# Running the W1 and wo matmuls as pairs of 64-row tiles, and moving N into the W2 stretches

## The chip, the cores and the metric

The kernel runs on one core of one Trainium2 chip. The metric is device time in microseconds (us), lower is better. PE is TensorE (the matmul engine), PEld its weight loads, ACT ScalarE, DVE VectorE, POOL GpSimd, SP the engine that issues most DMAs. A kernel's time is the median of its runs; single runs of one kernel differ by up to 1.3%, and a good part of this study is about telling such noise from effects.

## The reference

One transformer layer on 2048 rows of width 576, in bf16. First a linear-attention mixer with 32 heads of 18 channels, then a channel MLP of width 4608:

```python
h  = x + A(layernorm(x))          # q, k, v; softmax feature maps; kv and z; num / den; then @ wo
h2 = h + B(layernorm(h))

def A(x):                         # cut: q, k, v per head, phi_q and phi_k are softmaxes of both signs
    num = phi_q @ kv              # "N" below: numerator and denominator of the attention
    den = phi_q @ z + 1e-6
    return (num / den) @ wo       # wo: 576 x 576

def B(x):
    y = layernorm(x)
    return gelu(y @ w1 + b1) @ w2 + b2    # w1: 576 x 4608, w2: 4608 x 576
```

## The kernel before

Rows are taken in 16 tiles of 128 (`t`). After a first phase (keys, values, the kv sums, queries) comes a loop of 8 rounds, `r = 0..7`, each with two tiles. A round has a W1 stretch (36 blocks `m` of hidden units for 256 rows, then gelu on ACT) and a W2 stretch (two tiles). N, wo and the second layernorm of the next round's two tiles, `a` and `b`, are put in between.

The contraction length of W1 and wo is 576 = 4 x 128 + 64. The four full chunks are ordinary 128-row matmuls. The remainder of 64 rows is done in W1 as two 64-row matmuls at a time, one on the upper and one on the lower half of the array (`h = 0` and `h = 64`), and in wo padded with zeros to 128 rows.

```python
def w1_group(r, g, off=0, n=RW):            # four blocks m, two PSUM banks
    b0 = 2 * (g % 2)
    where = [(4 * g + i, b0 + i // 2, 512 * (b0 + i // 2) + RW * (i % 2)) for i in range(4)]
    for i in (0, 2, 1, 3):                  # tails: 64 rows, two at a time
        m, bk, o = where[i]; h = 64 * (i // 2); w = 128 * (2 * g + i % 2)
        P.add("pe", matmul(ps_all[:, o:o + n], w1t[h:h + 64, w:w + 128], yT[h:h + 64, 4, ys], ...), banks=[bank[bk]])
    for m, bk, o in where:                  # full chunks: 128 rows
        for c in range(4):
            P.add("pe", matmul(ps_all[:, o:o + n], w1sb[:, c, 128 * m:128 * m + 128], yT[:, c, ys], ...), banks=[bank[bk]])
    ...                                     # four gelus on ACT

def attn_wo(t, bset, early=False):
    for c in range(5):                      # 512 + 64 output columns, 128 rows
        for (bk, o, n) in ((A, 0, 512), (C, 512, 64)): ...
    ...                                     # DVE: residual, sums; POOL: power; DVE: norm; transposing DMA

def w2_tile(r, j, slots):
    for i in range(NF + LAG):               # NF = 36; per m 512 columns in bank mb, 64 columns in bank 4
        if i in slots: slots[i]()
        ...
    P.add("pool", tmpo = x_all[t] + b2)     # b2 addition, emitted after the tile
    ...                                     # DVE: ostage = PSUM + tmpo; DMA out

for r in range(NR):
    for g in range(NG):
        w1_group(r, g)
        if more and r and g == 0: attn_N(a, S1)
        if more and g == 5:       attn_wo(a, S1)
        if more and g == 6:       attn_N(b, S1)
    slots = {24: attn_wo(b, S1)} if more
    w2_tile(r, 0, slots); w2_tile(r, 1, {})
```

The softmax here doesn't subtract the row's maximum and nothing guards it: scores larger than these inputs give would overflow.

## Time and profile before

| | before |
|---|---|
| time, median of the first 4 runs | 440.04 us (439.58 to 440.81) |
| profiled span | 437.4 us |
| PE busy | 95% |
| a steady round (r = 1 to 6) | 41.10 us |
| of it the W1 stretch (one wo, two N inside) | 21.77 us |
| of it the W2 stretch (one wo inside) | 19.33 us |
| the last round's W1 (nothing inside) | 19.39 us |

A stretch is measured from its first weight load to that of the next stretch. From the page: the span; PE's busy time, share and instructions; the chain of work that ended last, by engine and by line; and two of the costliest groups (L839: full W1 matmuls, L833: W1 tails; columns: busy us and mean ns of one, then idle time before them). In the chain, "issue" is time in which an engine waited for nothing that the profile shows, and a name with q is an engine's sequencer, which issues its instructions.

```profile
span 437.4 us, 8921 instructions
PE 415.1 (95%) x3685; PEld 265.3 (61%) x3685; DVE 186.8 (43%) x461; ACT 183.1 (42%) x406; POOL 94.8 (22%) x120
PE 81%; DVE 10%; issue 3%; ACT 2%; DMA 2%; POOL 1%; SPq 1%; DVEq 0%; ACTq 0%
PE ps_all L839 31%; PE ps_all L862 26%; PE ps_all L833 5%; PE ps_all L684 4%; PE ps_all L599 4%; PE ps_all L534 4%; PE ps_all L519 3%; DVE ybuf L380 2%; PE ps_all L629 2%; DMA RA<-in_A_wqkv_dram 2%; PE ps_all L569 2%; DVE tpn L693 1%; SPq L330 1%; POOL st L701 1%; DVE bns L366 1%
...
L839 PE MATMUL ps_all<-yT,w1sb 128*128 128x256 bf16 x1152 | 138.2, 273 | 0.0
...
L833 PE MATMUL ps_all<-yT,w1t 64*128 64x256 bf16 x288 | 28.2, 274 | 2.0 <-ACT yT L618 2.0
```

PE is the bound, and W1 and W2 are most of it. But "busy" does not say whether a matmul's time was used: the records overlap, one lasts 273 ns while a new one starts every 109 ns. What the groups cost must be read from starts. The timeline of PE in one steady W1 stretch (start us, length us, then line and operation, merged):

```profile
198.15 0.39 PE L833 MATMUL ps_all<-yT,w1t 64*128 64x256 bf16 x4
...
198.47 1.92 PE L839 MATMUL ps_all<-yT,w1sb 128*128 128x256 bf16 x16
...
200.33 0.39 PE L833 MATMUL ps_all<-yT,w1t 64*128 64x256 bf16 x4
```

One group takes 200.33 - 198.15 = 2.18 us. Its matmuls fill 18 slots of 109 ns (16 full ones and two pairs of tails), 1.97 us. The single records show where the other 0.21 us is (ns from start to start):

```
full -> full                 109
last full -> first tail      205     change from 128-row to 64-row matmuls
tail -> other tail of a pair   3     the two halves of the array run together
  -> first tail of next pair 116     or 117; so 119 or 120 from pair to pair
  -> other tail of that pair   3
last tail -> first full      202     change back
first full -> second full    119
```

So each change between 128-row and 64-row matmuls costs about 0.1 us: 93 to 96 ns in its own gap, and 10 or 11 more in the next. There are two per group and 72 groups.

Another cause is at hand: the tails of a group also wait for ACT, which must have emptied their bank, and the view names ACT before many of them. But of the 44 groups that follow a full matmul directly, it names ACT for 31 and nothing for 13, and the gap is the same 0.21 us, as in these two weight loads:

```profile
111.58 0.11 PEld L833 LDWEIGHTS ps_all<-yT,w1t 64*128 64x128 bf16 x4 [0.21 <-issue]
113.76 0.12 PEld L833 LDWEIGHTS ps_all<-yT,w1t 64*128 64x128 bf16 x4 [0.21 <-ACT RA L844]
```

So the gap is not a wait for ACT; experiment 3 tests this without ACT. The Trainium skill, "TensorEngine Tiling (Array Packing)", section "Key Properties", says that a change of tiling mode drains TensorE; the pause at each change in the trace agrees, though it does not show the drain itself, and it gives the size, which the page does not.

### The profile page before, as it was taken

The numbers are of one execution on the slowest core, as the hardware profiler recorded it, in microseconds if no ns is written. First come the engines' busy times: TensorE is split into PE (matmuls) and PEld (weight loads), VectorE is DVE, ScalarE is ACT, GpSimd is POOL, SyncE is SP. The second block draws the span as 40 slices with busy tenths as digits, with TensorE's granted clock in tenths as the row PEclk, the third lists the DMA queues.
The fourth block names the chain that finished last, engine by engine and source line by source line (L and its number), as shares of the span: only waits on it lengthen the run. The fifth ranks groups of instructions, "written<-read, shape, count | busy, mean of one in ns | idle before, by whom it ended". The sixth has DMA issues, their size and how long they took to land.

```text
span 437.4 us, 8921 instructions
## 1 busy us (share of the span) xinstructions
PE 415.1 (95%) x3685; PEld 265.3 (61%) x3685; DVE 186.8 (43%) x461; ACT 183.1 (42%) x406; POOL 94.8 (22%) x120
## 2 busy tenths in 40 slices
PE   6679999886999999999999999999999999999996
PEld 2346666665774576467647755775576567646753
DVE  4598898787053125332334332452135322430000
ACT  1447775376870175026404620660175026404710
POOL 4179783001102111201121012102111201121000
PEclk9889999999999999999999999999999999999999
DMA  8689887400610100310310011101100100110000
GB/s 187 144 174 205 254 190 201 139 1 1 211 38 16 43 16 19 26 30 16 32 30 16 15 31 30 30 15 17 43 17 15 31 28 16 30 30 15 2 0 29
DMA packets 49265, 26.11 MB, mean 60 GB/s; under 512 B 37064, under 2 KB 48200, under 8 KB 49224
## 3 DMA queue, kind: packets, MB, share of 16 engines
q1 hardware_dynamic: 46912, 23.67, 23.4%
q10 hardware_dynamic: 2312, 1.86, 1.7%
q8 instruction: 29, 0.48, 0.5%
q14 instruction: 12, 0.10, 0.1%
HBM read 14.47 MB, written 2.36 MB: 38 GB/s over the span
## 4 chain that ended last, share of the span: by engine, by line
PE 81%; DVE 10%; issue 3%; ACT 2%; DMA 2%; POOL 1%; SPq 1%; DVEq 0%; ACTq 0%
PE ps_all L839 31%; PE ps_all L862 26%; PE ps_all L833 5%; PE ps_all L684 4%; PE ps_all L599 4%; PE ps_all L534 4%; PE ps_all L519 3%; DVE ybuf L380 2%; PE ps_all L629 2%; DMA RA<-in_A_wqkv_dram 2%; PE ps_all L569 2%; DVE tpn L693 1%; SPq L330 1%; POOL st L701 1%; DVE bns L366 1%
## 5 line engine op out<-in xcount | busy, mean ns | idle before, releaser
L844 ACT ACTIVATE RA<-ps_all,b1T 128x256 bf16<-128x256 f32 x288 | 122.5, 470 | 183.8 <-PE ps_all L839 174.1
L839 PE MATMUL ps_all<-yT,w1sb 128*128 128x256 bf16 x1152 | 138.2, 273 | 0.0
L839 PEld LDWEIGHTS ps_all<-yT,w1sb 128*128 128x128 bf16 x1152 | 106.8, 98 | 26.6 <-issue 15.2
L862 PE MATMUL ps_all<-w2a,RA 128*128 128x512 bf16 (+1 forms) x640 | 95.3, 286 | 0.7
L862 PEld LDWEIGHTS ps_all<-w2a,RA 128*128 128x128 bf16 x640 | 46.0, 98 | 38.6 <-DVE WQ L871 4.1
L862 PE MATMUL ps_all<-RB,RA 128*128 128x64 bf16 (+1 forms) x512 | 68.6, 286 | 0.0
L690 DVE SCALAR_TENSOR_TENSOR x_all<-ps_all,x_all 128x576 bf16<-128x576 f32 x16 | 12.1, 756 | 113.6 <-PE ps_all L684 113.6
L862 PEld LDWEIGHTS ps_all<-RB,RA 128*128 128x128 bf16 x512 | 33.5, 98 | 32.3
L871 DVE TENSOR_TENSOR WQ<-ps_all,tmpo 128x64 bf16<-128x64 f32 (+1 forms) x32 | 14.6, 455 | 86.2 <-PE ps_all L862 84.6
L665 POOL TENSOR_TENSOR obuf<-tpn 128x576 bf16<-128x576 f32 x14 | 19.6, 1401 | 110.8 <-DVE tpn L660 110.8
L701 POOL TENSOR_TENSOR st<-st,neghalf 128x1 f32<-128x1 f32 x16 | 8.8, 548 | 155.1 <-DVE st L703 155.1
L833 PE MATMUL ps_all<-yT,w1t 64*128 64x256 bf16 x288 | 28.2, 274 | 2.0 <-ACT yT L618 2.0
L868 POOL TENSOR_TENSOR tmpo<-x_all,b2bc 128x576 f32<-128x576 bf16 x16 | 20.4, 1273 | 43.6 <-DVE WQ L871 43.6
L605 ACT ACTIVATE Eq<-ps_all 128x512 bf16<-128x512 f32 (+1 forms) x48 | 25.3, 527 | 10.4 <-PE ps_all L599 9.5
L380 POOL TENSOR_SCALAR ybuf<-x_all,st 128x576 bf16<-128x576 bf16 x12 | 27.6, 2300 | 1.8 <-POOL st L360 0.9
L525 ACT ACTIVATE RB<-ps_all 128x576 bf16<-128x576 f32 x32 | 19.1, 647 | 20.4 <-PE ps_all L519 20.4
L599 PE MATMUL ps_all<-yT,WQ 128*128 128x256 bf16 x200 | 25.0, 273 | 0.2 <-ACT Eq L605 0.2
L519 PE MATMUL ps_all<-RA,yT 128*128 128x512 bf16 (+1 forms) x160 | 23.1, 293 | 1.4 <-ACT RB L525 1.3
L555 DVE TENSOR_TENSOR RB<-ps_all,RB 128x1152 bf16<-128x1152 f32 x16 | 21.5, 1346 | 6.8 <-PE ps_all L534 6.7
L534 PE MATMUL ps_all<-RB,yT 128*128 128x512 bf16 (+1 forms) x160 | 22.9, 291 | 0.3 <-DVE RB L555 0.3
L684 PE MATMUL ps_all<-wo_sb,OTR 128*128 128x512 bf16 (+1 forms) x160 | 22.2, 286 | 0.1
L544 DVE TENSOR_REDUCE sums<-RB 128x64 f32<-128x1152 bf16 x16 | 21.5, 1341 | 0.0
(86 smaller groups left out, 293.1 us busy)
## 6 DMA issues: line engine op xcount, KB each, us to landing
w1sb<-in_B_w_dram SPq DMA_DIRECT2D x8, 576.0 KB, 4.8
w2a<-in_B_w_dram SPq DMA_DIRECT2D x4, 720.0 KB, 6.8
RB<-in_B_w_dram SPq DMA_DIRECT2D x2, 1152.0 KB, 7.6
out_dram<-WQ SPq DMA_DIRECT2D x16, 144.0 KB, 1.9
x_all<-in_A_x_dram SPq DMA_DIRECT2D x2, 576.0 KB, 4.7
RB<-in_A_wqkv_dram ACTq DMA_DIRECT2D x1, 576.0 KB, 5.8
x_all<-in_A_x_dram ACTq DMA_DIRECT2D x1, 576.0 KB, 7.9
w1t<-in_B_w_dram SPq DMA_DIRECT2D x2, 288.0 KB, 4.0
```

The source lines that it names most:

```text
L380: P.add(eng, lambda e: e.tensor_scalar(ybuf[yb][:, 0:D], src, mean, rstd, ALU.subtract, ALU.mult), reads=[r_src, *r_st], writes=[res(f"ybu ...
L519: P.add("pe", lambda e, c=c, o=o, n=n: e.matmul(ps_all[:, 512 * KB + o:512 * KB + o + n], yT[:, c, sl * 128:(sl + 1) * 128], weffk[:, c, o ...
L534: P.add("pe", lambda e, c=c, o=o, n=n: e.matmul(ps_all[:, 512 * VB + o:512 * VB + o + n], yT[:, c, sl * 128:(sl + 1) * 128], wv[:, c, o:o ...
L544: P.add("dve", lambda e: e.tensor_reduce(sums[vb][:, :], Ek[eb][:, 0:1152].rearrange("p (h f) -> p h f", h=64), AX.X, ALU.add), reads=[res ...
L555: P.add("dve", lambda e: e.tensor_tensor(vx(t)[:, :, :, 0:DH], ps_all[:, 512 * VB:512 * VB + D].rearrange("p (h d) -> p h d", h=H).unsquee ...
L599: P.add("pe", lambda e, i=i, c=c, h0=h0: e.matmul(ps_all[:, 512 * bk + RW * i:512 * bk + RW * i + RW], weffq[:, c, DH * h0:DH * h0 + 128], ...
L605: P.add("act", lambda e, s=s: e.activation(Eq[:, r, s, bs[0]:bs[0] + n, :], ps_all[:, 512 * bk:512 * bk + RW * n].rearrange("p (b t) -> p ...
L684: P.add("pe", lambda e, c=c, bk=bk, o=o, n=n: e.matmul(ps_all[:, 512 * bk:512 * bk + n], oT[ob][:, c, :], wo_sb[:, c, o:o + n], start=(c = ...
L833: P.add("pe", lambda e, i=i, o=o, h=h, w=w: e.matmul(ps_all[:, o:o + n], w1t[h:h + 64, w:w + 128], yT[h:h + 64, 4, ys], start=(i % 2 == 0) ...
L839: P.add("pe", lambda e, c=c, m=m, o=o: e.matmul(ps_all[:, o:o + n], w1sb[:, c, 128 * m:128 * m + 128], yT[:, c, ys], start=False, stop=(c ...
L844: P.add("act", lambda e, m=m, o=o: e.activation(hmid[:, m, off:off + n], ps_all[:, o:o + n], AF.Gelu_apprx_tanh, bias=b1T[:, m:m + 1]), re ...
L862: P.add("pe", lambda e, m=m, bk=bk, o=o, n=n: e.matmul(ps_all[:, 512 * bk:512 * bk + n], w2_lhs(m, j), w2_rhs(m, o, n), start=(m == 0), st ...
```

## The change

The intent: run all of W1 as 64-row matmuls, so that the mode no longer changes inside it. Every 128-row matmul becomes two 64-row ones, on the upper and lower half of the array, that run at once. Two halves at work must not write one PSUM bank (the Trainium skill, same page, "Gotcha 1: PSUM Pressure", says so and leaves it to software), so at any time the two lanes work on unlike units (a unit is two blocks `m` in one bank), and semaphores hold back a lane that takes over a bank from the other. A "takeover" below is that: the first matmul of a lane on a unit whose other half the other lane has just done.

The same is done for wo, whose 576 output columns now lie as 288 + 288 in two banks. Both wo of a round go into W1 (they no longer change the mode there). Both N, whose matmuls are 128-row ones, go from W1 to W2. The core of the diff:

```diff
+    def wo_half(t, bset, step):              # lanes pe0 (rows 0-63) and pe8 (rows 64-127), unlike banks
+        lo = [one("pe0", step, 0, c, ...) for c in cs]
+        hi = [one("pe8", 1 - step, 64, c, ...) for c in cs]      # N=288, 5 + 4 pairs in two steps
@@ attn_N
+        P.add(oeng, obuf[:, 576:640] = tpn[:, 0, 512:576] + tpn[:, 1, 512:576])   # copy of the last 64 columns
@@ W1
-    def w1_group(...)
+    UBANK = ...                              # 18 units over banks 0 to 4
+    SKEW = 3
+    def w1_round(r, extra):
+        for s in range(NF // 2):
+            k = s % 3
+            u8 = s + (2, -1, -1)[k]          # pe0: units 0,1,2,...   pe8: units 2,0,1,...
+            lo += w1_half(r, s, 0, k < 2)
+            hi += w1_half(r, u8, 64, k == 0)
+            ...                              # gelus of finished units; extra: halves of wo
+        hi = [(None, None)] * SKEW + hi      # program order: pe0 matmul i+3, then pe8 matmul i
@@ w2_tile
-        mb = 2 + (RT * r + j) % 2
+        mb = (3, 2)[j]
+        for ... in (64 columns, 512 columns)[::1 - 2 * j]:   # second tile: DVE evicts the 512-column bank first
@@ rounds
+            ia, ib = (3, 12) if r else (9, None)          # wo(a), wo(b): after W1 steps 3, 4 and 12, 13
+            if r == 0:
+                extra[4] = attn_N(b); slots[0][8] = attn_wo(b, S1, True)
+        if r + 2 < NR:
+            slots[0][16 if r == 0 else 2] = attn_N(a + RT)
+            slots[1][6 if r else 12] = attn_N(b + RT)
```

(Shortened; the bookkeeping gives each lane its own semaphore and makes a lane wait for the other where they touch the same bank.)

More of the change, by code (lines that the diff above doesn't have):

```diff
@@ L12 @@
 ENG_PIDS = ("pe", "act", "dve", "pool", "sp")
+LANES = ENG_PIDS + ("pe0", "pe8")
 ENG_ATTR = {"pe": "tensor", "act": "scalar", "dve": "vector", "pool": "gpsimd", "sp": "sync"}
 class Res:
-    __slots__ = ("name", "w", "r", "strict")
+    __slots__ = ("name", "w", "r")
     def __init__(self, name=""):
         self.name = name
-        self.strict = name.startswith("junk")
         self.w = None
@@ L50, in __init__ @@
         self.ops = {p: [] for p in ENG_PIDS}
+        self.lane = {p: [] for p in LANES}
         self.seen = {p: {} for p in ENG_PIDS}
@@ L57, in _need, with _collect @@
             waits[tok[0]] = tok[1]
-    def _collect(self, eng, reads, writes, banks):
+    def _collect(self, lane, reads, writes, banks):
         waits = {}
-        inorder = eng == "pe"
+        pe = lane in ("pe", "pe0", "pe8")
         for r in reads:
@@ L64, in _collect @@
         for w in writes:
-            if w.w is not None and (w.strict or not (inorder and w.w[0] == eng)):
-                self._need(waits, w.w)
-            for pid, v in w.r.items():
-                if not (inorder and pid == eng):
-                    self._need(waits, (pid, v))
+            self._need(waits, w.w)
+            for tok in w.r.items():
+                self._need(waits, tok)
         for b in banks:
             for pid, v in b.last.items():
-                if pid != eng:
+                if {pid, lane} == {"pe0", "pe8"} or not (pid == lane or pe and pid[:2] == "pe"):
                     self._need(waits, (pid, v))
@@ L77, in _plan_waits @@
         for pid, v in sorted(waits.items()):
-            if v <= 0 or (eng == "pe" and pid == "pe"):
-                continue
-            if self.seen[eng].get(pid, 0) >= v:
+            if v <= 0 or self.seen[eng].get(pid, 0) >= v:
                 continue
@@ L83, in _plan_waits @@
             self.seen[eng][pid] = v
-            if pid in ENG_PIDS:
-                self.ops[pid][v - 1].inc_needed = True
+            if pid in LANES:
+                self.lane[pid][v - 1].inc_needed = True
     @staticmethod
@@ L96, in _mark, with add @@
             b.last[tok[0]] = tok[1]
-    def add(self, eng, fn, reads=(), writes=(), banks=()):
+    def add(self, lane, fn, reads=(), writes=(), banks=()):
+        eng = lane[:2] if lane in ("pe0", "pe8") else lane
         op = _Op(fn)
-        self._plan_waits(eng, self._collect(eng, reads, writes, banks), op)
-        op.inc_sem = eng
+        self._plan_waits(eng, self._collect(lane, reads, writes, banks), op)
+        op.inc_sem = lane
         self.ops[eng].append(op)
-        self._mark((eng, len(self.ops[eng])), reads, writes, banks)
+        self.lane[lane].append(op)
+        self._mark((lane, len(self.lane[lane])), reads, writes, banks)
     def chan(self, name, eng):
@@ L134, in emit @@
         vals = {}
-        for pid in ENG_PIDS:
+        for pid in LANES:
             count = 0
             vl = [0]
-            for op in self.ops[pid]:
-                if op.inc_needed and op.inc_sem == pid:
+            for op in self.lane[pid]:
+                if op.inc_needed:
                     count += 1
@@ L155, in body @@
                     for (wpid, wv) in op.waits:
-                        v = vals[wpid][wv] if wpid in ENG_PIDS else wv
+                        v = vals[wpid][wv] if wpid in LANES else wv
                         engine.wait_ge(sems[wpid], v)
@@ L160, in body @@
                     ins = op.fn(engine)
-                    if op.inc_sem in ENG_PIDS:
+                    if op.inc_sem in LANES:
                         if op.inc_needed:
@@ L479, in _build @@
     P.add("dve", lambda e: e.memset(weffq[:, :, 576:592], 0.0), writes=[res("weffqpad"), res("warm")])
-    P.add("dve", lambda e: e.memset(wo_sb[64:128, 4, :], 0.0), writes=[res("wopad")])
-    for i in range(2):
-        P.add("dve", lambda e, i=i: e.memset(obuf[i][:, D:640], 0.0), writes=[res(f"opad{i}")])
     bulk = []
@@ L497, in _build @@
     add_bulk(wo_sb[:, 0:4, :], A_wo[0:512, :].rearrange("(c p) m -> p c m", p=128), [res("wo")])
-    add_bulk(wo_sb[0:64, 4, :], A_wo[512:576, :], [res("wo4")])
+    DHF = D // 2
+    for k in range(2):
+        add_bulk(wo_sb[64 * k:64 * k + 64, 4, 0:DHF], A_wo[512:576, DHF * k:DHF * k + DHF], [res("wo4")])
     NW2A = NF - NW2B
@@ L666, in attn_N @@
               reads=[res("tpn")], writes=[res(f"obuf{ob}")])
+        P.add(oeng, lambda e: e.tensor_tensor(obuf[ob][:, D:640], tpn[:, 0, 512:D], tpn[:, 1, 512:D], ALU.add),
+              reads=[res("tpn")], writes=[res(f"opad{ob}")])
         if oeng == "pool":
@@ L677, in attn_oT, with one @@
             pe_tr(obuf[ob], oT[ob], bset, rd, wr)
+    def wo_half(t, bset, step):
+        A, C, B = bset
+        ob = t % 2
+        def one(lane, k, h, c, first, last):
+            bk = (A, C)[k]
+            o = 0 if c == 4 else DHF * k
+            P.add(lane, lambda e: e.matmul(
+                ps_all[:, 512 * bk:512 * bk + DHF], oT[ob][h:h + 64, c, :], wo_sb[h:h + 64, c, o:o + DHF],
+                start=first, stop=last, skip_group_check=True),
+                reads=[res(f"oT{ob}"), res("wo"), res("wo4")], banks=[bank[bk]])
+        cs = (4, 0, 1, 2, 3) if step == 0 else (0, 1, 2, 3)
+        lo = [lambda c=c: one("pe0", step, 0, c, c == 4, step == 1 and c == 3) for c in cs]
+        hi = [lambda c=c: one("pe8", 1 - step, 64, c, c == 4, step == 1 and c == 3) for c in cs]
+        return lo, hi
     def attn_wo(t, bset, early=False):
         A, C, B = bset
-        ob = t % 2
-        for c in range(5):
-            for (bk, o, n) in ((A, 0, 512), (C, 512, 64)):
-                P.add("pe", lambda e, c=c, bk=bk, o=o, n=n: e.matmul(
-                    ps_all[:, 512 * bk:512 * bk + n], oT[ob][:, c, :], wo_sb[:, c, o:o + n],
-                    start=(c == 0), stop=(c == 4)),
-                    reads=[res(f"oT{ob}"), res("wo"), res("wo4"), res("wopad")], banks=[bank[bk]])
+        if early:
+            for step in range(2):
+                for a, b in zip(*wo_half(t, bset, step)):
+                    a()
+                    b()
         w = res(f"s2_{t}")
@@ L690, in attn_wo @@
         P.add("dve", lambda e: e.scalar_tensor_tensor(
-            x_all[:, t, :], ps_all[:, 512 * A:512 * A + D], 0.0, x_all[:, t, :], ALU.add, ALU.add,
-            accum_out=st(0)), reads=[res(f"x{t}")], writes=[res(f"x{t}"), w], banks=[bank[A], bank[C]])
+            x_all[:, t, :].rearrange("p (k d) -> p k d", k=2),
+            hap(ps_all, PR, 512 * A, [[512 * (C - A), 2], [1, DHF]]), 0.0,
+            x_all[:, t, :].rearrange("p (k d) -> p k d", k=2), ALU.add, ALU.add, accum_out=st(0)), reads=[res(f"x{t}")], writes=[res(f"x{t}"), w], banks=[bank[A], bank[C]])
         P.add("dve", lambda e: e.scalar_tensor_tensor(
@@ L705, in attn_wo @@
         yb = norm("dve", x_all[:, t, :], res(f"x{t}"), st(6), st(5), (res(f"s2f_{t}"), res(f"s2e_{t}")), True)
-        if not early:
+        if t >= RT:
             tr_y(yb, t)
@@ L777, in _build @@
         bulk.pop(0)()
-    ps_kv = lambda off, dims: hap(ps_all, PR, off, dims, 126)
+    ps_kv = lambda off, dims: hap(ps_all, PR, off, dims)
     P.add("dve", lambda e: e.tensor_tensor(
-        kvr[0:126, :, 0:25, 0:19], ps_kv(512 * 5, [[512, 2], [19, 25], [1, 19]]),
-        mask25[0:126, :, :].unsqueeze(1).to_broadcast([126, 2, 25, 19]), ALU.mult),
+        kvr[:, :, 0:25, 0:19], ps_kv(512 * 5, [[512, 2], [19, 25], [1, 19]]),
+        mask25[:, :, :].unsqueeze(1).to_broadcast([128, 2, 25, 19]), ALU.mult),
         reads=[res("mask25")], writes=[res("kvr")], banks=[bank[5], bank[6]])
     P.add("dve", lambda e: e.tensor_tensor(
-        kvr[0:126, :, 25:32, 0:19], ps_kv(512 * 7, [[133, 2], [19, 7], [1, 19]]),
-        mask7[0:126, :, :].unsqueeze(1).to_broadcast([126, 2, 7, 19]), ALU.mult),
+        kvr[:, :, 25:32, 0:19], ps_kv(512 * 7, [[133, 2], [19, 7], [1, 19]]),
+        mask7[:, :, :].unsqueeze(1).to_broadcast([128, 2, 7, 19]), ALU.mult),
         reads=[res("mask7")], writes=[res("kvr")], banks=[bank[7]])
@@ L821, in _build @@
     ch_out = [P.chan(f"out{i}", "sp") for i in range(2)]
-    def w1_group(r, g, off=0, n=RW):
-        b0 = 2 * (g % 2)
-        y0 = yts(r).start + off
-        ys = slice(y0, y0 + n)
-        yr = yrs(r)[off // 128:(off + n) // 128]
-        where = [(4 * g + i, b0 + i // 2, 512 * (b0 + i // 2) + RW * (i % 2)) for i in range(4)]
-        for i in (0, 2, 1, 3):
-            m, bk, o = where[i]
-            h = 64 * (i // 2)
-            w = 128 * (2 * g + i % 2)
-            P.add("pe", lambda e, i=i, o=o, h=h, w=w: e.matmul(
-                ps_all[:, o:o + n], w1t[h:h + 64, w:w + 128],
-                yT[h:h + 64, 4, ys], start=(i % 2 == 0), stop=False, skip_group_check=True),
-                reads=R_w1t + yr, banks=[bank[bk]])
-        for m, bk, o in where:
-            for c in range(4):
-                P.add("pe", lambda e, c=c, m=m, o=o: e.matmul(
-                    ps_all[:, o:o + n], w1sb[:, c, 128 * m:128 * m + 128],
-                    yT[:, c, ys], start=False, stop=(c == 3), skip_group_check=True),
-                    reads=[res(f"w1_{c}_{m // 18}")] + yr, banks=[bank[bk]])
-        for m, bk, o in where:
-            P.add("act", lambda e, m=m, o=o: e.activation(
-                hmid[:, m, off:off + n], ps_all[:, o:o + n], AF.Gelu_apprx_tanh, bias=b1T[:, m:m + 1]),
-                reads=[res("b1T")], writes=[res(f"hm{m}_{j}") for j in range(off // 128, (off + n) // 128)] +
-                (RA_OLD if r == 0 else []), banks=[bank[bk]])
@@ new lines, in _build, with w1_half, one @@
+    UNITS = [(4 * (u // 2) + u % 2, 4 * (u // 2) + u % 2 + 2) for u in range(NF // 2)]
+    UBANK = {}
+    for k in range(0, NF // 2, 3):
+        for i, u in enumerate((k, k + 2, k + 1)):
+            UBANK[u] = (k + i) % 5
+    def w1_half(r, u, h, begin):
+        lane = "pe8" if h else "pe0"
+        ys, yr, bk = yts(r), yrs(r), UBANK[u]
+        def one(i, c, first):
+            m = UNITS[u][i]
+            o = 512 * bk + RW * i
+            if c == 4:
+                w = 128 * (2 * (m // 4) + m % 2)
+                lhs, rd = w1t[h:h + 64, w:w + 128], R_w1t
+            else:
+                lhs, rd = w1sb[h:h + 64, c, 128 * m:128 * m + 128], [res(f"w1_{c}_{m // 18}")]
+            P.add(lane, lambda e: e.matmul(ps_all[:, o:o + RW], lhs, yT[h:h + 64, c, ys],
+                                           start=first, stop=not begin and i == 1 and c == 3, skip_group_check=True),
+                  reads=rd + yr, banks=[bank[bk]])
+        k = 1 if h else 0
+        return [lambda i=i, c=c, n=n: one(i, c, begin and n == 0)
+                for n, (i, c) in enumerate([(k, 4)] + [(i, c) for i in (0, 1) for c in range(4)])]
@@ new lines, in w1_act @@
+    def w1_act(r, u):
+        for i, m in enumerate(UNITS[u]):
+            o = 512 * UBANK[u] + RW * i
+            P.add("act", lambda e, m=m, o=o: e.activation(
+                hmid[:, m, :], ps_all[:, o:o + RW], AF.Gelu_apprx_tanh, bias=b1T[:, m:m + 1]),
+                reads=[res("b1T")], writes=[res(f"hm{m}_{j}") for j in range(RT)] +
+                (RA_OLD if r == 0 else []), banks=[bank[UBANK[u]]])
+    SKEW = 3
+    def w1_round(r, extra):
+        lo, hi = [], []
+        for s in range(NF // 2):
+            k = s % 3
+            u8 = s + (2, -1, -1)[k]
+            lo += [(f, None) for f in w1_half(r, s, 0, k < 2)]
+            hi += [(f, None) for f in w1_half(r, u8, 64, k == 0)]
+            if k == 1:
+                hi.append((None, lambda s=s: w1_act(r, s - 1)))
+            if k == 2:
+                hi.append((None, lambda s=s: (w1_act(r, s), w1_act(r, s - 1))))
+            for fl, fh, after in extra.get(s, ()):
+                lo += [(f, None) for f in fl]
+                hi += [(f, None) for f in fh]
+                if after:
+                    hi.append((None, after))
+        hi = [(None, None)] * SKEW + hi
+        n8 = 0
+        while lo or n8 < len(hi):
+            if lo:
+                f = lo.pop(0)[0]
+                f()
+            while n8 < len(hi):
+                f, g = hi[n8]
+                if f is None and g is not None:
+                    g()
+                    n8 += 1
+                    continue
+                if f is not None:
+                    f()
+                n8 += 1
+                break
+            while n8 < len(hi) and hi[n8][1] is not None:
+                hi[n8][1]()
+                n8 += 1
@@ L869, in w2_tile @@
               reads=[res("b2"), res(f"x{t}")], writes=[res("tmpo"), res("maskf")])
-        for bk, o, n in ((TAILB, 512, 64), (mb, 0, 512)):
+        for bk, o, n in ((TAILB, 512, 64), (mb, 0, 512))[::1 - 2 * j]:
             P.add("dve", lambda e, bk=bk, o=o, n=n: e.tensor_tensor(
@@ L875, in w2_tile @@
               reads=[res(f"ostage{ob}")])
-    NG = NF // 4
     for r in range(NR):
         a, b = RT * (r + 1), RT * (r + 1) + 1
-        more = r + 1 < NR
-        for g in range(NG):
-            w1_group(r, g)
-            if more and r and g == 0:
-                attn_N(a, S1)
-            if more and g == 5:
-                attn_wo(a, S1)
-            if more and g == 6:
-                attn_N(b, S1)
-        slots = {}
-        if more:
-            slots[24] = lambda b=b: attn_wo(b, S1)
-        w2_tile(r, 0, slots)
-        w2_tile(r, 1, {})
+        extra, slots = {}, ({}, {})
+        if r + 1 < NR:
+            ia, ib = (3, 12) if r else (9, None)
+            for t, i in ((a, ia), (b, ib)):
+                if i is not None:
+                    extra[i] = [(*wo_half(t, S1, 0), None)]
+                    extra[i + 1] = [(*wo_half(t, S1, 1), lambda t=t: attn_wo(t, S1))]
+            if r == 0:
+                extra[4] = [((), (), lambda: attn_N(b, S1))]
+                slots[0][8] = lambda: attn_wo(b, S1, True)
+        if r + 2 < NR:
+            slots[0][16 if r == 0 else 2] = lambda: attn_N(a + RT, S1)
+            slots[1][6 if r else 12] = lambda: attn_N(b + RT, S1)
+        w1_round(r, extra)
+        w2_tile(r, 0, slots[0])
+        w2_tile(r, 1, slots[1])
     P.final_dma_waits("sp")
```

## The prediction

> **What bounds the kernel now.** TensorE. The page gives PE 95% of the 437.4 us span; the chain of waits is 81% PE (30.5% full W1 matmuls, 25.5% W2, 5.4% W1 tails). In the waits view PE's stalls (about 18 us in all) lie before the steady rounds. Six steady rounds take 41.1 us each (in the chain, 150.34 to 396.94): in the windows view W1 with one wo and two N takes 21.7, W2 with the other wo 19.3. ScalarE (13.9 of 21.7 in W1) is not the limit.
>
> In the trace's single matmuls, full W1 matmuls start every 109 ns. A group of 16 plus four 64-row tails takes 2.176 us, though 18 slots of 109 are 1.966. The rest is two changes between 128- and 64-row matmuls: about 200 ns from start to start in place of 109, and 10 more in the next gap, near 0.1 us each. The Trainium skill, "TensorEngine Tiling (Array Packing)", Key Properties, says that changing the tiling mode drains TensorE; the 200 ns gaps agree. 72 groups x 0.206 = 14.8 us, all on the critical path.
>
> **What the change does to the sum.**
> - Array work is equal: 9 slots a unit. In the tail pairs the second tile starts 3 ns after the first, both weight loads under the running matmuls. Expected: pairs every 109-112 ns.
> - Removed: 14.8 us of changes. Left per W1 stretch: two changes (8 x 0.2) and a skew of three slots (8 x 0.33): net -10.6.
> - wo: 1.22 us inserted before; now nine paired slots of N=288, about 1.1. 14 in the loop: -1.7.
> - wo out of W2: the gap at the change of W2 tiles (475 ns against 216, behind VectorE's eviction) goes in steady rounds: -1.8.
> - N (0.6 us each) only moves.
> - Lane waits: a dependent matmul comes four slots (436 ns) after the one it needs, whose record lasts 272 ns: free, unless signalling takes over 100 ns.
> - Against it, round 0: wo(3) and N(4) sit in W2 tile 0, N(5) in tile 1. GpSimd runs in order, so the b2 addition (1.27 us) queues behind N's output addition, 6 us after N starts. Estimated stalls: 2.2 us in tile 1, 0.7 in the next W1, 0.4 of extra changes, 0.6 because ScalarE needs 1.99 us per four gelus in round 0 against 1.97 of matmul.
> - Before the loop: 0.4 for the copied columns and mode changes.
>
> Sum: -9.8 us at 109 ns a slot. Each ns above adds 1.3 us; allowing a little, 431.5 us.
>
> **What would show each step.** Single matmuls in W1: pair spacing near 109 ns, no 200 ns gaps inside; W1 stretch near 20.4 us with two wo; W2 near 18.9 with two N; a steady round 39.3 to 39.8. The waits view: a new PE wait of 2-3 us in round 0 for VectorE's eviction (W2's 64-column matmuls). PE waits for its own lanes near zero.
>
> **What would make it wrong.** Instruction delivery: W1 needs a load and a matmul every 54 ns for 18 us on end; before has that pace only in bursts (52.7 ns over 10, 83 over 60). A slot of 120 ns would take all the gain (+14 us). Lane signals slower than 436 ns would stall twelve times a round. Round 0 stalling less would make it faster: about 428.
>
> Chances: faster by over 2% (under 431.6) 0.48, within 2% 0.44, slower 0.08. Range 426 to 438.

## The result

| | before | after |
|---|---|---|
| time, median of 4 runs | 440.04 us | 427.91 us (427.46 to 430.21) |
| ratio after / before | | 0.9733 (95%: 0.9695 to 0.9771) |
| a steady round (after: r = 2 to 5) | 41.10 us | 39.12 us |
| W1 stretch of a steady round | 21.77 us | 20.23 us |
| W2 stretch of a steady round | 19.33 us | 18.90 us |
| the last round's W1 | 19.39 us | 18.02 us |
| first round, W1 and W2 | 21.19, 19.34 us | 20.00, 22.36 us |
| first W1 load to last matmul | 324.4 us | 312.6 us |

Ratios are the mean time of one kernel's fast runs over that of the other's of the same rounds, so they are not quite the ratio of the medians quoted. The kernel became 2.7% faster; 431.5 us was predicted, with a range of 426 to 438. The lines of the page after (L860 is W1, L928 W2, L688 wo):

```profile
span 426.3 us, 11565 instructions
PE 396.8 (93%) x4924; PEld 287.1 (67%) x4965; DVE 182.9 (43%) x460; ACT 175.3 (41%) x406; POOL 98.3 (23%) x134
...
L860 PE MATMUL ps_all<-yT,w1sb 64*128 64x256 bf16 x2304 | 152.2, 269 | 0.0
...
L860 PE MATMUL ps_all<-yT,w1t 64*128 64x256 bf16 x288 | 71.5, 270 | 2.5 <-ACT yT L617 2.0
...
L688 PE MATMUL ps_all<-wo_sb,OTR 64*128 64x288 bf16 x288 | 29.4, 283 | 0.3
```

The number of matmuls on W1's full chunks doubled (1152 to 2304), and PE's busy time fell. The same steady round in both kernels, before and after, in the view by windows (stretch, its length, busy us and count of instructions for PE, PEld, DVE, ACT, POOL, then granted clock, DMA share and GB/s). Before, W1 and W2:

```profile
232.14:253.91 21.77, 21.77 (x213) 16.43 (x211) 10.07 (x33) 13.91 (x34) 1.95 (x2) 1.00 0.11 24
253.91:273.25 19.34, 19.24 (x157) 9.81 (x155) 4.56 (x12) 1.17 (x3) 4.46 (x4) 1.00 0.11 25
```

After:

```profile
231.85:252.08 20.23, 20.23 (x363) 19.04 (x361) 6.13 (x20) 12.38 (x32) 1.09 (x2) 1.00 0.08 20
252.08:270.98 18.90, 18.58 (x161) 10.29 (x165) 7.87 (x24) 1.61 (x5) 5.82 (x6) 1.00 0.14 32
```

The last round's W1, in which nothing is inserted, before and after:

```profile
396.54:415.93 19.39, 19.39 (x182) 14.38 (x180) 0.92 (x2) 13.80 (x34) 1.27 (x1) 1.00 0.03 10
387.19:405.21 18.02, 18.02 (x327) 17.16 (x324) 0.92 (x2) 12.16 (x32) 1.27 (x1) 1.00 0.04 11
```

Weight loads are busy 19.0 of 20.2 us in W1 now, at full clock, and still the pairs start every 109 ns: delivering a load and a matmul every 54 ns for a whole stretch is no limit here. That was the largest risk named.

The new waits of PE in the loop, after (total us, times, longest; one more lies before the loop, for DVE at L412, 1.3 us here and 0.8 us in a second profile of the same kernel):

```profile
PE ps_all L928 <- DVE WQ L937: 1.9, 1, 1.9
...
PE ps_all L928 <- ACT RA L871: 1.1, 7, 0.2
...
PE ps_all L860 <- DVE WQ L937: 0.6, 1, 0.6
```

The first and the last are the stalls of the first round that were predicted. Their cause can be read in the timeline around them, in order of time:

```profile
141.26 1.40 POOL L664 TENSOR_TENSOR obuf<-tpn 128x576 bf16<-128x576 f32 x1 [4.59 <-issue]
142.62 0.32 POOL L666 TENSOR_TENSOR obuf<-tpn 128x64 bf16<-128x64 f32 x1
142.90 1.27 POOL L934 TENSOR_TENSOR tmpo<-x_all,b2bc 128x576 f32<-128x576 bf16 x1
144.30 0.95 DVE L937 TENSOR_TENSOR WQ<-ps_all,tmpo 128x64 bf16<-128x64 f32 x2 [3.17 <-POOL tmpo L934]
144.59 1.67 PE L928 MATMUL ps_all<-w2a,RA 128*128 128x64 bf16 x13 [1.93 <-DVE WQ L937]
```

N's output additions (L664, L666) hold POOL; the b2 addition (L934) stands behind them in POOL's order, although its data had been there all along; DVE's eviction waits for it; and PE waits for the bank.

The middle line of the waits, seven times 0.16 us for ACT at the start of W2, is not real. There the first W2 weight load starts 198 ns after the last W1 matmul, as at any change of mode, and the second load 15 ns later; the first W2 matmul ran between, but its record is missing (the page counts 623 of 640), so the gap looks longer by one matmul.

### The profile page after: what moved, and what is told of

Same layout as the page of the kernel before. It is cut to its first block, busy times and chain, and to the rows that moved or that the text cites. A ratio compares the mean times of both kernels' runs of the same rounds, so it can differ in the third digit from the quotient of the medians.

```text
span 426.3 us, 11565 instructions
## 1 busy us (share of the span) xinstructions
PE 396.8 (93%) x4924; PEld 287.1 (67%) x4965; DVE 182.9 (43%) x460; ACT 175.3 (41%) x406; POOL 98.3 (23%) x134
## 4 chain that ended last, share of the span: by engine, by line
PE 61%; issue 2%; ACT 1%; POOL 1%; DVE 0%; ACTq 0%; DVEq 0%
PE ps_all L928 29%; PE ps_all L860 28%; PE ps_all L688 4%; PE ps_all L628 1%; ACT RA L871 1%; POOL tmpo L934 1%; DVE WQ L937 0%; POOL obuf L664 0%; POOL obuf L666 0%; ACTq L157 0%; DVEq L157 0%
## 5 line engine op out<-in xcount | busy, mean ns | idle before, releaser
L871 ACT ACTIVATE RA<-ps_all,b1T 128x256 bf16<-128x256 f32 x288 | 114.8, 478 | 180.2 <-PE ps_all L860 165.4
L860 PE MATMUL ps_all<-yT,w1sb 64*128 64x256 bf16 x2304 | 152.2, 269 | 0.0
L860 PEld LDWEIGHTS ps_all<-yT,w1sb 64*128 64x128 bf16 x2304 | 135.4, 94 | 6.2
L928 PE MATMUL ps_all<-w2a,RA 128*128 128x64 bf16 (+1 forms) x623 | 93.9, 284 | 3.9 <-DVE WQ L937 1.9
L860 PE MATMUL ps_all<-yT,w1t 64*128 64x256 bf16 x288 | 71.5, 270 | 2.5 <-ACT yT L617 2.0
L928 PEld LDWEIGHTS ps_all<-w2a,RA 128*128 128x128 bf16 x640 | 45.8, 98 | 37.9 <-DVE WQ L937 2.2
L928 PE MATMUL ps_all<-RB,RA 128*128 128x64 bf16 (+1 forms) x499 | 66.7, 284 | 0.4
L928 PEld LDWEIGHTS ps_all<-RB,RA 128*128 128x128 bf16 x512 | 33.4, 98 | 32.4
L707 DVE SCALAR_TENSOR_TENSOR x_all<-ps_all,x_all 128x576 bf16<-128x576 f32 x16 | 12.1, 757 | 83.0 <-PE ps_all L688 83.0
L664 POOL TENSOR_TENSOR obuf<-tpn 128x576 bf16<-128x576 f32 x14 | 19.6, 1401 | 92.3 <-DVE tpn L659 81.2
L934 POOL TENSOR_TENSOR tmpo<-x_all,b2bc 128x576 f32<-128x576 bf16 x16 | 20.3, 1271 | 43.2 <-DVE WQ L937 43.2
L688 PE MATMUL ps_all<-wo_sb,OTR 64*128 64x288 bf16 x288 | 29.4, 283 | 0.3
L860 PEld LDWEIGHTS ps_all<-yT,w1t 64*128 64x128 bf16 x288 | 26.3, 94 | 4.7 <-ACT yT L617 2.1
L524 ACT ACTIVATE RB<-ps_all 128x576 bf16<-128x576 f32 x32 | 19.1, 647 | 20.5 <-PE ps_all L518 20.5
L533 PE MATMUL ps_all<-RB,yT 128*128 128x64 bf16 (+1 forms) x154 | 21.6, 287 | 0.3
```

Of the source, the lines that this page charges most:

```text
L533: P.add("pe", lambda e, c=c, o=o, n=n: e.matmul(ps_all[:, 512 * VB + o:512 * VB + o + n], yT[:, c, sl * 128:(sl + 1) * 128], wv[:, c, o:o ...
L664: P.add(oeng, lambda e: e.tensor_tensor(obuf[ob][:, 0:D], tpn[:, 0, :], tpn[:, 1, :], ALU.add), reads=[res("tpn")], writes=[res(f"obuf{ob}")])
L688: P.add(lane, lambda e: e.matmul(ps_all[:, 512 * bk:512 * bk + DHF], oT[ob][h:h + 64, c, :], wo_sb[h:h + 64, c, o:o + DHF], start=first, s ...
L860: P.add(lane, lambda e: e.matmul(ps_all[:, o:o + RW], lhs, yT[h:h + 64, c, ys], start=first, stop=not begin and i == 1 and c == 3, skip_gr ...
L871: P.add("act", lambda e, m=m, o=o: e.activation(hmid[:, m, :], ps_all[:, o:o + RW], AF.Gelu_apprx_tanh, bias=b1T[:, m:m + 1]), reads=[res( ...
L928: P.add("pe", lambda e, m=m, bk=bk, o=o, n=n: e.matmul(ps_all[:, 512 * bk:512 * bk + n], w2_lhs(m, j), w2_rhs(m, o, n), start=(m == 0), st ...
```

## The experiments

Twelve kernels were run. Two things disturb their total times. One is short: PE's granted clock falls to half for one or a few periods of 3.4 us before the loop and, in some executions, also once at the start of the first W1 stretch. The Trainium skill, "TensorE: Matmul & The Clock Gate", Part 1, describes such a gate with a window of that length; the traces agree, with half-clock periods of 3.41, 6.83 or 10.24 us before the loop. Here is one execution of a kernel met below (early b2, second time), the clock in the third number from the end:

```profile
109.00:113.00 4.00, 2.02 (x26) 1.67 (x24) 3.16 (x11) 3.04 (x6) 0.35 (x1) 1.00 0.01 2
113.00:117.40 4.40, 4.40 (x54) 3.62 (x51) 0.00 (x0) 1.76 (x4) 1.33 (x2) 0.61 0.32 52
```

Where it falls on the first W1 stretch, that takes 21.67 us in place of 20.00. The other is the first weights' DMA, for which PE waited 5.3 to 8.6 us in these profiles. The profile of the kernel before shows both as well (half clock at 13.0 and 26.7 us, and 6.5 us of waiting). So the verdicts below rest on stretches of the loop after the first W1, which repeat to 0.01 us from execution to execution, and the totals are given beside them.

The theories. **A**: the gain is the mode changes that W1 no longer makes; moving wo and N only makes that possible. **B**: the gain is the new place of wo and N, through shorter W2 stretches. **C**: 64-row matmuls are cheaper in themselves; this one the trace of after refutes without a run, since pairs start every 109 ns, as full matmuls did.

### 1. W1 alone put back (w1old)

The changed kernel with the old `w1_group`, wo in pairs beside the tails, N in W2:

```diff
-    def w1_round(r, extra): ...              # lanes
+    def w1_round(r, extra):
+        for g in range(NF // 4):
+            w1_group(r, g)                   # as before: 128-row matmuls and tails
+            for s in (2 * g, 2 * g + 1): ... # the halves of wo, in pairs
```

> The changed kernel with W1 alone put back to 128-row matmuls and paired tails; wo stays in 64-row pairs (placed beside the tails), N stays in W2. Theory A (the gain is the mode changes inside W1): the last round's W1 stretch goes from 18.02 back to about 19.4 us, 8 rounds x 1.37 = +11 us, so about 439 us, nearly the old time. Theory B (the gain is where wo and N stand, so that W2 no longer waits): the time stays within 3 us of 427.9.

Measured: 441.47 us, ratio to before 1.0032 (1.0002 to 1.0061). The last round's W1:

```profile
399.40:418.79 19.39, 19.39 (x182) 14.36 (x180) 0.91 (x2) 13.94 (x34) 1.27 (x1) 1.00 0.03 10
```

That is the old 19.39 us to the digit, against 18.02 after. The new places of wo and N without the new W1 gain nothing in all: a steady round is 0.25 us shorter than before (21.86 + 18.99 us) and the W2 of r = 6 is 1.5 us shorter (17.84 us), but the first round's W2 takes 22.46 us where it took 19.34. By itself B is not the cause of the gain.

### 2. wo and N alone put back (wonback)

```diff
-            ia, ib = (3, 12) if r else (9, None) ...
+            if r: extra[1] = attn_N(a)
+            extra[10], extra[11] = the halves of wo(a)
+            extra[13] = attn_N(b)
+            slots[0][24] = attn_wo(b, S1, True)
```

> W1 stays in 64-row pairs, but N goes back into W1 and the second wo back into W2, so three insertions a round change the mode in and out, and the gap at the W2 tile change returns. Theory A: a steady round goes from 39.12 to about 40.0 us (6 changes x 0.1 plus 0.26); the first round loses its 2.5 us stall, so about 430.5 us in all. Theory B: the steady round goes back to about 41 us and the time to about 438 us.

Measured: 437.48 us (435.34 to 440.14), ratio 0.9945 (0.9884 to 1.0006). A steady round took 40.37 us:

```profile
236.37:257.15 20.78, 20.78 (x365) 18.22 (x362) 9.79 (x32) 12.61 (x33) 2.23 (x3) 1.00 0.11 25
257.15:276.74 19.59, 19.41 (x163) 9.79 (x162) 4.84 (x13) 1.52 (x5) 4.75 (x5) 1.00 0.13 25
```

The direction is A's, the size is not: 1.25 us a round above after, where 0.88 was expected. The total missed the expected one by 7 us. Six rounds of 0.37 us make 2.2 of that. The seventh round (r = 6) lost 1.3 us waiting for a transposing DMA of wo's input (waits view), which the kernel before does not do. Its W2 took 19.59 us, with a wo inside, where that of after took 17.75 with nothing left to put in: 1.84 us more, when the other rounds lose 0.69 there, so 1.2 us that the expectation left out. A half-clock stretch on the first W1 makes 1.7 in the profiled execution; the rest is not traced.

So the two parts of the change are not additive. From the first W1 load to the last matmul, with the half-clock stretch of the first W1 (21.67 - 20.00 us) taken off where it fell, the new W1 alone (this run) is 5.3 us shorter than before, the new places alone (w1old) 0.3 us longer, and both together 11.8 us shorter. So the new W1 alone gives less than half of the gain; 6.5 us come only when the places change with it. Of the 6.8 us by which the parts fall short of the sum, 1.3 are the DMA wait of the seventh round. A reason for the rest can be read from the stretches, though no run tests it alone: beside 128-row matmuls N was inserted without any change of mode (in before an N added 0.57 us, which is its own length), and beside pairs it needs two. Moving N did not pay by itself; it kept the pairs from paying.

### 3. What a mode change costs by itself (dummy128, dummy64)

Into the changed kernel's W1, nine times a round, one idle matmul of 64 columns into a spare bank; once with 128 rows, once with 64 rows:

```diff
+    def dummy(r):
+        P.add("pe",  matmul(ps_all[:, 2560:2624], w1sb[:, 0, 0:128], yT[:, 0, 64 columns], ...))      # dummy128
+        P.add("pe0", matmul(ps_all[:, 2560:2624], w1sb[0:64, 0, 0:128], yT[0:64, 0, ...], ...))       # dummy64
+            if s % 2: hi.append((None, lambda: dummy(r)))
```

> After every second step of W1 one idle 128-row matmul of 64 columns into a spare bank (9 a round, 72 in all). If a mode change costs 0.1 us each way, each insertion costs about 0.23 us: +17 us, about 445 us. If the cost of a mode change is hidden in lanes that run apart, it is near +2 us as in the run with 64-row dummies.

> The control: the same 72 dummies as 64-row matmuls on the first row tile, so without a mode change. Expected cost 0 to 30 ns each: 428 to 430 us. If this costs as much as the 128-row dummies, then any extra instruction, and not the mode change, is what costs.

Measured: 449.72 us and 432.54 us, ratios 1.0231 and 0.9827. W1 of a steady round, first dummy128, then dummy64:

```profile
241.33:263.67 22.34, 22.34 (x372) 18.62 (x370) 6.13 (x20) 12.72 (x33) 1.10 (x2) 1.00 0.09 18
```

```profile
234.21:254.67 20.46, 20.46 (x372) 19.65 (x369) 6.13 (x20) 12.38 (x32) 1.09 (x2) 1.00 0.09 20
```

A 64-row dummy costs (20.46 - 20.23) / 9 = 26 ns, which is its 64 columns. The same dummy with 128 rows costs (22.34 - 20.23) / 9 = 234 ns. The difference, 0.208 us for two changes, is what a group of before lost (0.21 us). Besides, the first dummy waits 2.3 us for the spare bank, which N still uses in the first round (waits view); both share that. With it the loop is accounted for: from the first W1 load to the last matmul, dummy128 is 19.1 us longer than after and dummy64 4.1, where 72 dummies and the wait make 19.2 and 4.2. In the timed runs dummy128 is 2.7 us slower still, before the loop or in the spread. A stands, and with its size.

### 4. The order of the lanes (skew0, skew1, skew2, skew8)

The prediction took 0.33 us a stretch for the second lane's lag of three slots, and held the lane waits for free. `SKEW = 3` was set to 0, 1, 2 and 8.

```diff
-    SKEW = 3
+    SKEW = 0     # 1, 2, 8
```

> The lag of the second lane is 0 pairs in place of 3: a matmul that takes over a bank from the other lane comes one slot (109 ns) after the one it waits for, 12 times a round. If a lane signal takes about 40 ns after the end of the matmul's record (272 ns; 40 ns is what VectorE needed to start after N's last matmul), each takeover stalls about 0.2 us: W1 of the last round +2.1 us, about +17 us in all, 445 us. If lanes need no real wait (signal before the pipeline's end), the time falls by 2.6 us to about 425.

> Lag of 1 pair: takeover two slots (218 ns) after its source. With a signal at about 312 ns from the matmul's start the stall is about 94 ns x 12 a round x 8 = 9.0 us, less 0.22 us of lag a round: about 435 us. Without real waits: about 426.

> Lag of 2 pairs: takeover three slots (327 ns) after its source. With a signal at about 312 ns nothing stalls and each W1 stretch is one slot shorter: 18.02 to 17.91 us in the last round, -0.9 us in all, about 427.0. If the signal takes over 400 ns, the 12 takeovers a round stall by 70 ns or more: about 434 us.

> The second lane comes 8 pairs later in program order in place of 3. The traces show the second lane's first matmul 13 ns after the first lane's, although three matmuls of the first lane stand before it in the program. If each row tile takes its own matmuls as soon as it can and only waits hold back what stands behind them, the last round's W1 stays at 18.02 us and the time at 428. If program order sets the lag, W1 becomes 5 slots longer, 18.57 us, and the time about 432 us.

Measured:

| pairs of lag in the program | time, us | ratio to before | last round's W1, us |
|---|---|---|---|
| 0 | 436.56 | 0.9921 (0.9893 to 0.9949) | 19.44 |
| 1 | 431.10 | 0.9812 (0.9780 to 0.9844) | 18.24 |
| 2 | 427.64 | 0.9731 (0.9706 to 0.9755) | 18.02 |
| 3 (after; two sets of runs) | 427.91, 429.49 | 0.9733, 0.9761 | 18.02 |
| 8 | 442.28 | 1.0060 (1.0035 to 1.0085) | 19.95 |

The expectations were half right. Lags 0 and 1 do stall, but less than expected; a lag of 2 is not one slot shorter than 3; and 8 takes the whole gain away, by neither of the two ways thought of. The records of the last round's W1 show what happens, in ns from its first matmul (the updates are the semaphore's own records):

```
                                                   SKEW 0   SKEW 3   SKEW 8
second lane's first matmul starts                       3       13      564
first lane ends its half of unit 0: last start        883      884      884
   its semaphore is updated                          1166     1167     1167
   the second lane's load that waits for it starts   1208     1209     1612
second lane ends its half of unit 2: last start       886     1063     1610
   its semaphore is updated                          1200     1503     2049
   start of the first-lane matmul just before it
   in program order                                   883     1212     1757
```

Three things follow.

1. *Starts are not in program order between the two halves.* With a lag of 3 the second lane's first matmul is the fifth in the program, and it started 13 ns after the first, before the three that stand between. With a lag of 8 it is the tenth, and it started at 564, just after the first lane's sixth (556), with three still pending before it. In both cases it passed three pending matmuls; with a lag of 3 there were no more to pass, with a lag of 8 it waited until only three were left. So a small `SKEW` in the program is not a lag on the chip.
2. *Signals are in program order.* A semaphore is updated about 283 ns after its matmul starts (or, with a lag of 0, 34 ns after the other lane's update just before it), unless an earlier matmul of the other lane has not finished: with a lag of 3, the matmul that started at 1063 signalled at 1503, 291 ns after the start (1212) of the one before it in the program. With a lag of 8 the update came at 2049, 292 ns after 1757, and the first lane's waiting load started at 2090, where its next slot was due at 1975. That is how a long lag hurts: the second lane's signals come late, and the first lane stands.
3. *A takeover takes 325 ns from the start of the matmul waited for to the start of the waiting load.* 283 ns to the update, 42 ns to the load; its matmul follows 4 ns later. With lags of 2 and 3 the second lane starts level with the first, and its first takeover starts at 1213 where level would be 993. (It had lost 0.15 us of that before, behind a wait for DVE's eviction of W2's bank, but the takeover could not have come sooner in any case.) From there on it trails by 0.23 us, each later takeover comes just in time, and it ends 0.23 us after the first lane. That is why 2 and 3 take the same time, and why the overhead is 0.23 us and not 0.33.

With a lag of 0 the waiting load also holds back the first lane's next matmul, which comes behind it in the program: both lanes start at 1212 and 1215, where 1102 was due, at each takeover.

The Trainium skill, "TensorE: Matmul & The Clock Gate", Part 3, "The mechanism", says that matmuls are in strict program order in start and end. For the ends (the signals) these runs agree. For starts on unlike halves of the array they do not, and the measurement decides.

### 5. No lag at the end (nolag)

If the 0.23 us come from the first takeover's wait, then work that lets takeovers come four or five slots after their source, and lets both lanes end together, should remove them. In six rounds the halves of wo were placed at unlike points of the lanes for this, on top of the early b2 addition of experiment 6:

```diff
+            elo = {2: a0l, 5: a1l, 8: b0l, 17: b1l}      # first lane: halves of wo(a), wo(b) after these W1 steps
+            ehi = {0: a0h, 3: a1h, 6: b0h, 9: b1h}       # second lane
+            skew = 0
```

(Cut: in these rounds DVE takes wo(b) out of other banks, 5 and 6, at the start of W2, and the first N moves from slot 2 of W2 to slot 8.)

> b2early, and in six rounds the halves of wo are set at unlike places in the two lanes, so that the takeovers always come 4 or 5 slots after their source and both lanes end together. If the second lane's lag of about 0.23 us at the end of W1 comes from waiting 325 ns at the first takeover, W1 of a steady round falls from 20.22 to about 20.0 us, and the time by 1.4 us to about 424 us. If the rest over 162 + wo slots has another cause (mode change, weight loads), W1 stays at 20.2.

Measured: 424.51 us, ratio 0.9649 (0.9626 to 0.9671). W1 of a steady round:

```profile
232.17:252.17 20.00, 20.00 (x363) 19.28 (x360) 4.37 (x11) 12.29 (x33) 1.79 (x2) 1.00 0.10 21
```

20.23 became 20.00 us, as the theory of the 0.23 us says; the last round of this kernel, which keeps the lag of 3, still took 18.02 us. But the output was wrong, with a relative error of 0.11: for wo(b) the lanes swap column halves, and the 64-row remainder of the weights lies with each half's columns on one half of the partitions only, so it met the wrong columns. This is read from the code. The same matmuls of the same shapes ran with the wrong weights, so the timing reading stands; the kernel cannot be used, and a mended one was not run.

### 6. The first round's stalls (b2early)

```diff
 def w2_tile(r, j, slots):
+    P.add("pool", tmpo = x_all[t] + b2)      # at the start of the tile, ahead of N's output addition
     for i in range(NF + LAG): ...
-    P.add("pool", tmpo = x_all[t] + b2)
```

> The addition of b2 on GpSimd is issued at the start of each W2 tile, ahead of N's output addition. If the first round's stalls come from GpSimd doing its work in order, as predicted (waits view: 1.9 us in W2, 0.6 us in the next W1 for VectorE's eviction), they go: the first round's W2 from 22.36 to about 20.4 us, the second round's W1 from 21.05 to about 20.3, about 425.3 us. If VectorE itself was too late, nothing changes.

Measured: 426.40 us, ratio 0.9707 (0.9677 to 0.9736). The first round's W2 fell from 22.36 to 20.48 us and the second round's W1 from 21.05 to 20.22; both of PE's waits for DVE's eviction are gone from the waits view. The timeline of the eviction in the first tile, to be held against that of after:

```profile
142.08 1.41 POOL L664 TENSOR_TENSOR obuf<-tpn 128x576 bf16<-128x576 f32 x1 [4.60 <-issue]
142.50 0.95 DVE L937 TENSOR_TENSOR WQ<-ps_all,tmpo 128x64 bf16<-128x64 f32 x2 [0.55 <-PE ps_all L932]
```

DVE now evicts while POOL is still busy with N's output; it waited for PE and no longer for POOL. In the traces this is 2.7 us.

To see whether it shows in the time, both kernels were run again in the same rounds on one chip:

> The changed kernel once more, so that it stands beside the next two on one chip and in the same rounds: about 428 us.

> The kernel with the early b2 addition, beside the changed kernel: by the traces its first two rounds are 2.7 us shorter, so about 425.3 us. If the earlier gain was only a difference of half-clock stretches before the loop, the two are equal.

Measured: 429.49 us, ratio 0.9761 (0.9737 to 0.9785), against 428.04 us, ratio 0.9728 (0.9695 to 0.9761). The early addition is ahead by 1.5 us here, and by as much in the first comparison (other chips), but the intervals overlap. The profiled execution of b2early_again had the half clock on its first W1 (21.67 us), and its single runs spread from 425.5 to 429.9. The removal of the stalls is shown by the stretches; that the whole program gains the full 2.7 us is not. It is the best version here with a right result.

## Why the prediction was right

The mechanism and the size were right; the time lay 3.6 us below the number and inside the range. Point by point:

| step | predicted | measured |
|---|---|---|
| a pair starts every 109 to 112 ns | 109 used, about 1.3 us allowed for more (440.04 - 9.8 = 430.2, against 431.5) | 109 ns; no allowance was needed |
| cost of one mode change | 0.1 us | 0.104 us (0.208 / 2, dummies) |
| W1's mode changes, less what is left | -10.6 us | 8 x (18.02 - 19.39) = -11.0 us |
| a wo in pairs | 1.1 us | (20.23 - 18.02) / 2 = 1.1 us |
| wo out of W2: the long gap at the change of W2 tiles goes | -1.8 us | gaps of 470 to 482 ns in 7 rounds before; after, none above 245 ns in six of them, 6 x 0.26 = 1.6 us |
| W1 with two wo | 20.4 us | 20.23 us |
| W2 with two N | 18.9 us | 18.90 us |
| a steady round | 39.3 to 39.8 us | 39.12 us |
| PE's stalls of the first round | 2.2 + 0.7 us | 1.9 + 0.6 us in the waits view; 1.9 + 0.8 removed by b2early |
| ACT's limit in the first W1 | 0.6 us | at most 0.1: 20.00 us, where 18.02, a wo of 1.10, an N of 0.57 and two changes of 0.1 make 19.9 |
| lane waits | free up to 436 ns, else twelve stalls a round | 325 ns: the second lane trails by 0.23 us after the first takeover, no stall later |

What was off, by size. The lag was taken as three slots because the program has three; it is what the first takeover makes it, 0.23 us. The lane waits were called free because a dependent matmul comes four slots after its source in the program. That reasoning failed: the lanes start level, the first takeover waits, and from then on the distance is the three slots that the handover needs. That `SKEW = 3` still stalled only once a stretch was in part luck; a lag of 1 or 8 would have stalled. The 0.6 us for ACT did not show; perhaps the five banks, in place of two pairs, give its longer gelus of the first round room enough, which no run tested. And about 1.3 us were allowed for pairs slower than 109 ns, which did not occur. From the first W1 load to the last matmul the program lost 11.8 us; the 0.4 us for the time before the loop cannot be told from the half-clock and DMA differences there. The rest of the 12.1 us in the timed runs is of the size of their own spread.

What the prediction did not see, although nothing in it hung on that, is how strongly the two parts depend on each other (experiments 1 and 2), and that program order does not order the starts on the two halves (experiment 4).

## What to carry to other kernels

Count the changes between full and 64-row matmuls in a dense PE stretch: here each cost 0.1 us, and splitting full matmuls into pairs to avoid the changes cost nothing in slots, even with twice the instructions. Once a stretch is in pairs, keep everything else out of it that would change the mode, or the gain goes back. Between lanes that hand over banks, keep the program distance just above the handover time (three slots of 109 ns for 325 ns; four were as good here) and not much longer, because signals come in program order; a lag of 8 took the whole gain, and lags of 4 to 7 were not run.

An engine that works in order and off the critical path still decides when a bank comes free: put the addition whose data is ready ahead of the one that has to wait.

## What the Trainium skill lacked or had wrong

- "TensorE: Matmul & The Clock Gate", Part 3, "The mechanism": it says that matmuls are in program order in start and end. Between the two 64-row halves a matmul started before three that stood ahead of it in the program (13 ns after the first one); with a program lag of 8 it started only when three were left before it (at 564 ns). The order of completion signals did follow the program.
- "TensorEngine Tiling (Array Packing)", "Key Properties": it names the drain at a change of tiling mode without its cost. Here 0.208 us for a change and the change back, by dummies with and without it; 0.21 us in a group of the kernel before.
- No page read here has the time of a handover between two row tiles of PE: 283 ns from a matmul's start (256 columns) to the semaphore's update, 42 ns more to the start of the waiting load.
- No page read here says that pairs of 64-row matmuls with a weight load each keep the full rate: a pair of 256 columns every 109 ns through stretches of 18 us, with the weight loads busy 94% of the time (19.04 of 20.23 us).
